# A fused attention and MoE kernel: the second last product as seven products of halves (Strassen), fused with the last one

## The chip, the cores and the metric

The kernel runs on one NeuronCore of one Trainium2 chip. A time is the device time of one execution in microseconds (us). The profile's span runs from the first to the last instruction of one profiled execution and is a little shorter than that execution's time. TensorE (PE in the profile) multiplies matrices; its weight loads are listed apart as PEld. VectorE is DVE, ScalarE is ACT, GpSimd is POOL, SyncE is SP; SP does no arithmetic here and only issues transfers between DRAM and the on-chip memory SBUF. TensorE writes its sums into PSUM, eight banks of 2 KB in each of 128 partitions.

## The reference, cut to what matters

```
p_packed = sm_attn(p, k, v)              # 8 batches, 8 heads, 576 tokens, head size 64
x = sm_attn(q, p_packed, p_packed)       # -> 4608 tokens x 512
x = ((x @ w1) * (x @ w2)) @ w3 @ w_out   # 512 -> 1024 -> 1024 -> 512
h = x @ w_in                             # 4608 x 512 times 512 x 2048: "the second last product"
g = where(h >= 1, h, where(h <= -1, 0, (h + 1)**2 / 4))
out = g @ w_out                          # 4608 x 2048 times 2048 x 512: "the last product"
```

The inputs are float64 or float32, the output is float32. To keep accuracy, each float32 operand of the large products is split into two float32r parts (high and rest), and three of the four products of parts are summed: `PASSES = ((0, 0), (0, 1), (1, 0))`. So one 128x128 piece of weights times one piece of activations costs three matmuls, each with its own weight load.

## The kernel before, in words

The order of the work is written out by hand on every engine; the framework only adds semaphores. There are three stretches.

**Start and batch 0** (to about 178 us): w3 and w_out of the first MoE are multiplied into one matrix, and batch 0 is worked off while weights arrive.

**Batches 1 to 7** (to 607 us): the loop `for b in range(1, B)`. Each batch has 24 units: 16 of `ab_unit` (12 matmuls of 288 columns each) and 8 of `x2_unit` (24 matmuls of 288 columns each), whose results go to the DRAM tensor `x2d`. The steps of the next batch's attention are put between the units. In batches 1 to 6 every fourth unit also calls `wd_convert`: it turns one 128x512 piece of the second MoE's float64 weights (32 pieces: 16 of `win`, 16 of `wout`) into float32 on ScalarE and VectorE and stores it to the DRAM tensor `wd`. In batch 7 the pieces are loaded again and split into their two parts (`wd_split`, one ScalarE and one VectorE instruction each, line 95 and 96), and they stay in SBUF to the end. `x2_block` loads and splits the 512 tokens of a block in the same way.

**The last stretch** (607 us to the end): nine blocks of `TB = 512` tokens, 16 steps each. Step i of a block computes 128 of the 2048 rows of h (`h_step`, line 642: 4 x 3 matmuls of 512 columns into one PSUM bank), and the activation: ScalarE `r` (line 648), VectorE maximum and multiply (lines 650 and 651), and one step later the split of the result into two parts, `g` (lines 95 and 96). Three steps later (`LAG = 3`) `out_step` (line 665) multiplies these parts by one 128-row piece of `wout`: 4 token chunks x 3 matmuls of 512 columns into four PSUM banks that collect over the 16 steps. So TensorE alternates 12 matmuls of `h` and 12 of `o`. At the end of a block ScalarE copies the four banks out (line 672) and issues their stores.

Engines run their queues in order: an instruction that waits holds up everything behind it on its engine. SP's queue of transfers is such a queue too.

Of the kernel before, what the change touches and what calls it, by code (L numbers as in the profile page):

```python
# [8 lines left out]
F32 = mybir.dt.float32  # L9
F32R = mybir.dt.float32r  # L10
# [3 lines left out]
AF = mybir.ActivationFunctionType  # L14
ALU = mybir.AluOpType
# [32 lines left out]
PASSES = ((0, 0), (0, 1), (1, 0))  # L48
# [3 lines left out]
def fused_kernel(ctx: ExitStack, tc, qT, kT, vv, pb, w1, w2, w3T, wo, win, wout, out):  # L52
    nc = tc.nc
# [373 lines left out]
    raw = {}  # L427
# [125 lines left out]
    def wd_load(i):
        if i >= 32:
            return
        if i < 16:
            n, k = divmod(i, 4)
            src = win[k * P:(k + 1) * P, n * 512:(n + 1) * 512]
        else:
            src = wout[(i - 16) * P:(i - 15) * P, :]  # L560
        raw[i] = load_weight(cv, src)

    def wd_convert(i):
        x = cv.tile([P, 512], F32, name="cvx", tag="cvx", bufs=2)
        for f in as_float32(cv, raw.pop(i), x):
            f()
        wd_load(i + 1)
        nc.sync.dma_start(out=wd[i], in_=x)
# [8 lines left out]
    def wd_split(i):
        pool = late["b1"] if i < 16 else late["b2"]
        f = late["b1"].tile([P, 512], F32, name="wf", tag="wf", bufs=3)
        nc.sync.dma_start(out=f, in_=wd[i])  # L580
        w_s[i] = pool.tile([P, 2, 512], F32R, name=f"ws{i}")
        return lambda: split(w_s[i], f)

    def x2_block(t, k):
        b1_, w = late["b1"], late["b1"] if t % 2 == 0 else late["b2"]
        f = b1_.tile([P, TB], F32, name="wf", tag="wf", bufs=3)
        t0 = t * TB
        nc.sync.dma_start(out=f, in_=x2d[t0 // XD][:, k, t0 % XD:t0 % XD + TB])
        x = w.tile([P, 2, TB], F32R, name=f"x2s{k}", tag=f"x2s{k}", bufs=1)
        split(x, f)  # L590
        x2_t[t, k] = x

    for b in range(1, B):
        if b + 1 < B:
            att, sa, bm = attention(b + 1)
            spread = dict(zip(EARLY, att))
            spread.update(zip(LATE, [bm[1, 0], bm[0, 0], sa[0], sa[1], bm[1, 1], bm[0, 1]]))
        else:
            spread = {}
            b1 = late["b1"] = tc.alloc_tile_pool(name="b1", bufs=1, side="left", reuse_waits="tile")  # L600
            todo = [wd_split(i) for i in range(2)]
        seq = []
        for f, n in ((ab_unit, 8), (x2_unit, 4)):
# [28 lines left out]
    todo = [wd_split(16 + i) for i in range(2)]  # L632

    g2_t = {}

    def h_step(t, i):
        ps = psB.tile([P, 512], F32, name="h", tag="h", bufs=2)
# [9 lines left out]
        r = b2.tile([P, TB], F32, name="r", tag="r", bufs=3)  # L647
        nc.scalar.activation(out=r, in_=ps[:, :TB], func=AF.Relu, scale=0.5, bias=half)  # L648
        m = b2.tile([P, TB], F32, name="mx", tag="mx", bufs=3)
        nc.vector.tensor_tensor(out=m, in0=ps[:, :TB], in1=r, op=ALU.max)  # L650
        nc.vector.scalar_tensor_tensor(out=m, in0=r, scalar=1.0, in1=m, op0=ALU.min, op1=ALU.mult)  # L651
        flush()
        g = b2.tile([P, 2, TB], F32R, name="g2", tag="g2", bufs=LAG + 2)
        g2_t[t, i] = g
        pend.append(lambda: split(g, m))

    acc = {}

    def out_step(t, i, cs=range(TB // P)):
        if i == 0:  # L660
            acc[t] = [psB.tile([P, 512], F32, name="o", tag="o", bufs=6) for _ in range(TB // P)]
        g = g2_t[t, i]
        for c in cs:
            for n, (s, v) in enumerate(PASSES):
                nc.tensor.matmul(  # L665
                    acc[t][c], g[:, s, c * P:(c + 1) * P], w_s[16 + i][:, v, :],
                    start=(i == 0 and n == 0), stop=(i == 15 and n == 2),
                )
        if i == 15:
            for c in cs:  # L670
                o = b2.tile([P, DM], F32, name="st", tag="st", bufs=2)
                nc.scalar.activation(out=o, in_=acc[t][c], func=AF.Copy)
                nc.scalar.dma_start(out=out[t * TB + c * P:t * TB + (c + 1) * P, :], in_=o)

    for s in range(16 * NB):
        t, i = divmod(s, 16)
        h_step(t, i)
        if t == 0:
            if i + 2 < 16:
                todo.append(wd_split(18 + i))  # L680
            todo.pop(0)()
        if t + 1 < NB and i >= 8 and i % 2 == 0:
            x2_block(t + 1, i // 2 - 4)
        if LAG <= s < 16 * NB:
            out_step(*divmod(s - LAG, 16))
# [62 lines left out]
```

## Time and profile before

| | us |
|---|---|
| median of three runs | 1402.66 (1401.42 to 1407.57) |
| the profiled execution's own time | 1402.18 |
| its span | 1400.4 |
| TensorE busy in the span | 1358.2 (97%) |
| VectorE busy | 683.9 (49%) |
| ScalarE busy | 477.3 (34%) |
| GpSimd busy | 0.7 |

The page of the profile gives each engine's busy time, the chain of work that ended last (followed back from the last instruction), and groups of instructions by source line with their count and mean duration. A matmul's recorded duration contains the time in which it runs through the array, and consecutive matmuls overlap in it: what one costs is the distance from its start to the next one's start, which the timeline gives. The timeline merges consecutive instructions of one line into a row with a count.

### The profile page before, as it was taken

The page shows a single profiled execution, that of the slowest core. Times are in us where ns is not written, and L with a number is a line of the kernel's source. Part 1 is how long each engine was busy: PE and PEld are TensorE (multiplying, and loading weights), DVE is VectorE, ACT ScalarE, POOL GpSimd, SP SyncE. Part 2 cuts the span into 40 slices and gives each one's busy share as a digit, 9 for nine tenths or more (in the row PEclk, how much of TensorE's full clock was granted, in tenths as well). Part 3 has the DMA queues.
Part 4 walks back from the last instruction along what each step waited for, and adds up shares of the span by engine and source line. Part 5 has one row for each costly group of instructions (what it writes and reads, how often), then busy time and mean ns, then how long its engine had stood idle before and what let it go on. Part 6 is the DMA issues. An engine that isn't in the chain of part 4 may idle for free.

```text
span 1400.4 us, 20204 instructions
## 1 busy us (share of the span) xinstructions
PE 1358.2 (97%) x8280; PEld 1122.6 (80%) x8280; DVE 683.9 (49%) x1269; ACT 477.3 (34%) x945; POOL 0.7 (0%) x6
## 2 busy tenths in 40 slices
PE   6699899999999999999999999999999999999998
PEld 2366688989888898988888888888888888888887
DVE  4684475666665664644434343343433433434332
ACT  3353253444535343533332222322222222222222
POOL 0000000000000000000000000000000000000000
PEclk9799999999999999999999999999999999999999
DMA  8763445536454521421100100001000010000000
GB/s 278 230 211 126 127 152 149 168 117 192 134 156 146 162 96 57 134 89 54 60 31 23 39 15 15 31 23 38 16 15 31 23 38 16 15 31 8 30 1 30
DMA packets 49788, 115.86 MB, mean 83 GB/s; under 512 B 5152, under 2 KB 16416, under 8 KB 47648
## 3 DMA queue, kind: packets, MB, share of 16 engines
q1 hardware_dynamic: 34144, 94.52, 22.1%
q10 hardware_dynamic: 15552, 20.06, 4.0%
q8 instruction: 65, 1.06, 0.3%
q14 instruction: 27, 0.22, 0.0%
HBM read 86.11 MB, written 28.44 MB: 82 GB/s over the span
## 4 chain that ended last, share of the span: by engine, by line
PE 86%; DMA 6%; DVE 4%; SPq 1%; issue 1%; ACT 1%; DVEq 0%; ACTq 0%
PE o L665 28%; PE h L642 28%; PE psk L370 12%; PE psk L394 11%; DMA raw<-win 2%; PE psk L478 2%; DMA raw<-w3T 2%; PE psk L186 2%; PE psm L175 1%; DMA raw<-wout 1%; DMA st<-x2d 1%; SPq L162 1%; PE psm L251 1%; PE psm L225 1%; DMA x2d<-st 1%
## 5 line engine op out<-in xcount | busy, mean ns | idle before, releaser
L665 PE MATMUL o<-ws,g 128*128 128x512 f32 x1728 | 417.7, 391 | 0.0
L642 PE MATMUL h<-x2s,ws 128*128 128x512 f32 x1728 | 417.5, 391 | 0.0
L665 PEld LDWEIGHTS o<-ws,g 128*128 128x128 f32 x1728 | 324.3, 188 | 70.9
L642 PEld LDWEIGHTS h<-x2s,ws 128*128 128x128 f32 x1728 | 324.3, 188 | 69.8 <-DVE x2s L96 0.4
L650 DVE TENSOR_TENSOR mx<-h,r 128x512 f32<-128x512 f32 x144 | 99.5, 691 | 450.2 <-ACT r L648 450.1
L648 ACT ACTIVATE r<-h,half 128x512 f32<-128x512 f32 x144 | 99.1, 688 | 531.5 <-PE h L642 528.2
L394 PEld LDWEIGHTS psk<-g,w 128*128 128x128 f32 x1500 | 200.4, 188 | 25.0 <-ACT st L421 20.7
L370 PE MATMUL psk<-at,m 128*128 128x288 f32 x1494 | 213.7, 298 | 3.8 <-DVE at L321 1.9
L370 PEld LDWEIGHTS psk<-at,m 128*128 128x128 f32 x1494 | 200.5, 188 | 18.2 <-issue 6.7
L394 PE MATMUL psk<-g,w 128*128 128x288 f32 x1500 | 208.8, 297 | 1.2 <-ACT st L421 1.2
L651 DVE SCALAR_TENSOR_TENSOR mx<-r,mx 128x512 f32<-128x512 f32 x144 | 99.7, 692 | 4.9
L96 DVE TENSOR_TENSOR g<-mx,g 128x512 fp32r<-128x512 f32 x144 | 98.4, 683 | 0.1
L382 DVE TENSOR_TENSOR tb<-psk,ta 128x288 f32<-128x288 f32 x124 | 56.3, 455 | 80.5 <-ACT ta L380 37.2
L95 ACT ACTIVATE g<-mx 128x512 fp32r<-128x512 f32 x144 | 89.6, 623 | 1.0 <-DVE mx L651 1.0
L478 PE MATMUL psk<-wo,w3f 128*128 128x512 f32 x128 | 62.7, 641 | 14.1 <-DVE w3f L127 14.1
L116 ACT ACTIVATE cvt<-raw 128x512 f32<-128x512 f32 x72 | 48.3, 675 | 66.7 <-DMA raw<-w 25.6
L380 ACT ACTIVATE ta<-psk 128x288 f32<-128x288 f32 x125 | 50.8, 407 | 51.0 <-PE psk L370 50.0
L478 PEld LDWEIGHTS psk<-wo,w3f 128*128 128x128 f32 x128 | 25.4, 207 | 46.4 <-issue 28.2
L96 DVE TENSOR_TENSOR g<-tb,g 128x288 fp32r<-128x288 f32 x128 | 57.2, 447 | 3.5 <-ACT g L95 2.8
L95 ACT ACTIVATE g<-tb 128x288 fp32r<-128x288 f32 x128 | 56.3, 440 | 6.1 <-DVE tb L382 5.7
L96 DVE TENSOR_TENSOR m<-psk,m 128x512 fp32r<-128x512 f32 x60 | 38.5, 683 | 34.7 <-ACT m L95 34.7
L421 ACT ACTIVATE st<-psk 128x288 f32<-128x288 f32 x61 | 24.8, 406 | 59.7 <-PE psk L394 57.9
(72 smaller groups left out, 602.9 us busy)
## 6 DMA issues: line engine op xcount, KB each, us to landing
x2d<-st ACTq DMA_DIRECT2D x72, 144.0 KB, 2.6
qk<-kT SPq DMA_DIRECT2D x8, 1152.0 KB, 12.3
qk<-qT SPq DMA_DIRECT2D x8, 1152.0 KB, 6.6
wf<-x2d SPq DMA_DIRECT2D x36, 256.0 KB, 2.7
out<-st ACTq DMA_DIRECT2D x36, 256.0 KB, 2.0
raw<-w3T SPq DMA_DIRECT2D x16, 512.0 KB, 5.1
raw<-w SPq DMA_DIRECT2D x16, 512.0 KB, 4.3
raw<-win SPq DMA_DIRECT2D x16, 512.0 KB, 3.9
```

Source lines behind the costliest of these rows:

```text
L95: nc.scalar.activation(out=dst[:, 0], in_=src, func=AF.Copy)
L96: nc.vector.tensor_tensor(out=dst[:, 1], in0=src, in1=dst[:, 0].bitcast(F32), op=ALU.subtract)
L370: nc.tensor.matmul(ps[w][:, :HS], m_tile[b, w, n][:, s, G, c0 * P:(c0 + 1) * P], at_tile[b][:, G, v, hf * HS:(hf + 1) * HS], start=(k == 0 ...
L380: nc.scalar.activation(out=bs, in_=ps[1][:, :HS], func=AF.Copy)
L382: nc.vector.tensor_tensor(out=g, in0=ps[0][:, :HS], in1=bs, op=ALU.mult)
L394: nc.tensor.matmul(ps, w34[kt][:, s, mt * P:(mt + 1) * P], g_t[kt, hf][:, v, :], start=(kt == kts[0] and n == 0), stop=(kt == kts[-1] and ...
L478: nc.tensor.matmul(acc[4 * hf + m], w3f[hf, j][:, m * P:(m + 1) * P], wof[j], start=(j == 0), stop=(j == 7))
L642: nc.tensor.matmul(ps[:, :TB], w_s[4 * n + k][:, s, c0 * P:(c0 + 1) * P], x2_t[t, k][:, v, :], start=(j == 0), stop=(j == 11),)
L648: nc.scalar.activation(out=r, in_=ps[:, :TB], func=AF.Relu, scale=0.5, bias=half)
L650: nc.vector.tensor_tensor(out=m, in0=ps[:, :TB], in1=r, op=ALU.max)
L651: nc.vector.scalar_tensor_tensor(out=m, in0=r, scalar=1.0, in1=m, op0=ALU.min, op1=ALU.mult)
L665: nc.tensor.matmul(acc[t][c], g[:, s, c * P:(c + 1) * P], w_s[16 + i][:, v, :], start=(i == 0 and n == 0), stop=(i == 15 and n == 2),)
```

## The change

The second last product takes, in every block, the matrices in halves: h's two halves of rows, the two halves of the sum's index (512 = 2 x 256), and two halves of 256 tokens (`TH`). Instead of eight products of halves it makes seven, named `A11, S1, A12, S2, S4, S3, A22`, from sums and differences of the quarters of `w_in` and of x (Strassen's scheme in Winograd's form).

- **The products.** A block now has 8 steps in place of 16; a step makes 2 x 128 rows of h. `product` is 6 matmuls of 256 columns (2 pieces x 3 passes), 42 in a step. Three products start a PSUM bank half (`x`, `z`, `y`); the other four add to `x` or `z` after a copy of what stood there was taken: `m1`, `m5`, `u2` on ScalarE. VectorE adds these copies to the banks to make three of the four quarters of the step's h, ScalarE copies the fourth.
- **The last product.** `out_part` is 3 matmuls of 512 columns. The 8 parts (24 matmuls) of step s-1 are placed between the products of step s, in groups of 1, 2, 3 and 2. The activation now reads h from SBUF instead of PSUM.
- **The weights.** `weight_tasks` makes a list of up to 144 tasks, one for each unit of batches 1 to 6: the same 32 conversions, 44 splits (`w_parts`: ScalarE copy, GpSimd subtraction, store of 512 KB; 28 for the seven combinations of `w_in`, 16 for `wout`) and 16 sums or differences on GpSimd (`w_combine`). The parts lie in DRAM (`wid`, `wod`). All 14 parts tiles of `w_in` (1 MB each) are loaded once: six during batch 7, four (`RIGHT`, first half) as soon as batch 7's buffers come free, four more later. A piece of 1 MB of `wout`'s parts is loaded for every step, `wo_load(i + 1)` at the end of step i, into two buffers.
- **The tokens.** A block's 512 tokens come in one load of 1 MB (`x2_load`); seven combinations are split (`x2_parts`, ScalarE and VectorE) after four differences on GpSimd (`x2_combine`). For the next block these 11 tasks are spread over steps 4 to 7.

```diff
--- before.py
+++ after.py
...
+TH = TB // 2
+A11, S1, A12, S2, S4, S3, A22 = range(7)
+LEFT = (A11, S1, A12)
...
-    wd = [dram.tile([P, 512], F32, name=f"wd{i}") for i in range(32)]
+    wid = [[dram.tile([P, 2, 2, 512], F32, name=f"wi{i}{n}") for n in range(2)] for i in range(7)]
+    wod = [dram.tile([P, 2, 2, DM], F32, name=f"wo{i}") for i in range(8)]
...
+    def w_convert(key, nxt):
+        def f():
+            x = wx[key] = cv.tile([P, 512], F32, name="cvx", tag="cvx", bufs=4)
+            for f in as_float32(cv, raw.pop("w"), x):
+                f()
+            if nxt is not None:
+                w_raw(nxt)
+        return f
+    def w_parts(key, dst):
+        def f():
+            x = wx[key]
+            p = cv.tile([P, 2, 512], F32R, name="hl", tag="hl", bufs=1)
+            nc.scalar.activation(out=p[:, 0], in_=x, func=AF.Copy)
+            nc.gpsimd.tensor_tensor(out=p[:, 1], in0=x, in1=p[:, 0].bitcast(F32), op=ALU.subtract)
+            nc.sync.dma_start(out=dst, in_=p.bitcast(F32))
+        return f
+    def w_combine(key, a, b, op):
+        return lambda: nc.gpsimd.tensor_tensor(out=wx[key], in0=wx[a], in1=wx[b], op=op)
+    def weight_tasks():
...
+        lines = [[conv.pop(0) for _ in range(3)], [conv.pop(0)]]
+        for x, (k, n) in enumerate(groups):
+            q = {z: (x, z) for z in (11, 12, 21, 22)}
+            take = lambda m=1: [conv.pop(0) for _ in range(m) if conv]
+            part = lambda i, z: w_parts(q[z], wid[i][n][:, k])
+            lines.append([part(A11, 11), None, None])
+            lines.append([part(A22, 22), w_combine(q[22], q[21], q[22], ALU.add), None])
+            lines.append([part(A12, 12), None, None])
+            lines.append([part(S1, 22), w_combine(q[22], q[22], q[11], ALU.subtract),
+                          w_combine(q[21], q[11], q[21], ALU.subtract)])
+            lines.append([part(S2, 22), w_combine(q[12], q[12], q[22], ALU.subtract)] + take())
+            lines.append([part(S3, 21)] + take())
+            lines.append([part(S4, 12)] + take() + take())
+            for j in range(4 * x, 4 * x + 4):
+                lines.append([w_parts(("o", j), wod[j // 2][:, j % 2])] + take())
...
+    def wi_load(i, n):
+        t = wi_t[i, n] = late["b1" if i in LEFT else "b2"].tile([P, 2, 2, 512], F32R, name=f"wi{i}{n}")
+        nc.sync.dma_start(out=t.bitcast(F32), in_=wid[i][n])
...
+    def x2_load(t):
+        f = late["b1"].tile([P, 4, TB], F32, name="f", tag="f", bufs=1)
         t0 = t * TB
+        nc.sync.dma_start(out=f, in_=x2d[t0 // XD][:, :, t0 % XD:t0 % XD + TB])
+        for r in range(2):
+            for c in range(2):
+                x2f[10 * r + c + 11] = f[:, 2 * r:2 * r + 2, c * TH:(c + 1) * TH]
+    def x2_combine(dst, a, b):
+        return lambda: nc.gpsimd.tensor_tensor(out=x2f[dst], in0=x2f[a], in1=x2f[b], op=ALU.subtract)
+    def x2_parts(t, i, src):
+        def f():
+            x = late["b1"].tile([P, 2, 2, TH], F32R, name="x2s", tag="x2s", bufs=8)
+            x2_t[t, i] = x
+            nc.scalar.activation(out=x[:, 0], in_=x2f[src], func=AF.Copy)
+            nc.vector.tensor_tensor(out=x[:, 1], in0=x2f[src], in1=x[:, 0].bitcast(F32), op=ALU.subtract)
+        return f
+    def x2_tasks(t):
+        return [
+            x2_parts(t, A11, 11), x2_combine(11, 12, 11), x2_combine(12, 22, 12),
+            x2_parts(t, S1, 11), x2_parts(t, A12, 21),
+            x2_parts(t, S4, 22), x2_combine(22, 22, 11),
+            x2_parts(t, S2, 22), x2_combine(21, 21, 22),
+            x2_parts(t, S3, 12), x2_parts(t, A22, 21),
+        ]
...
+            x2_load(0)
+            for n in range(2):
+                for i in LEFT:
+                    wi_load(i, n)
+            x2_todo = x2_tasks(0)
...
             if b == B - 1:
+                for _ in range(2 if u >= 18 else 0):
+                    if x2_todo:
+                        x2_todo.pop(0)()
+            elif w_todo:
+                task = w_todo.pop(0)
+                if task:
+                    task()
...
+    def wo_load(i):
+        t = wo_t[i] = buf("wo")
+        nc.sync.dma_start(out=t.bitcast(F32), in_=wod[i])
+    RIGHT = [i for i in range(7) if i not in LEFT]
+    first["g2"] = buf("g2")
+    late_wi = []
+    for i in RIGHT[:2]:
+        t = wi_t[i, 1] = b2.tile([P, 2, 2, 512], F32R, name=f"wi{i}1")
+        late_wi.append((t, i))
+    for i in RIGHT:
+        wi_load(i, 0)
+    for tag in ("H", "r"):
+        first[tag] = buf(tag)
+    wo_load(0)
+    for tag in ("m1", "m5", "u2", "st"):
+        first[tag] = buf(tag)
+    for i in RIGHT[2:]:
+        t = wi_t[i, 1] = b2.tile([P, 2, 2, 512], F32R, name=f"wi{i}1")
+        late_wi.append((t, i))
+    for t, i in late_wi:
+        nc.sync.dma_start(out=t.bitcast(F32), in_=wid[i][1])
...
+    BANK = {A11: "x", S1: "z", A12: "y", S2: "x", S4: "z", S3: "x", A22: "x"}
...
+    def product(t, i, q):
+        b = BANK[q]
+        if q in (A11, S1, A12):
+            bank[b] = psB.tile([P, TH], F32, name=b, tag=b, bufs=2 if b == "x" else 1)
         n, c0 = divmod(i, 4)
         j = 0
-        for k in range(4):
+        for k in range(2):
             for s, v in PASSES:
                 nc.tensor.matmul(
-                    ps[:, :TB], w_s[4 * n + k][:, s, c0 * P:(c0 + 1) * P], x2_t[t, k][:, v, :],
-                    start=(j == 0), stop=(j == 11),
+                    bank[b], wi_t[q, n][:, k, s, c0 * P:(c0 + 1) * P], x2_t[t, q][:, v, k, :],
+                    start=(j == 0 and q in (A11, S1, A12)), stop=(j == 5), skip_group_check=True,
                 )
                 j += 1
...
+    def copy(tag, b):
+        c = buf(tag)
+        nc.scalar.activation(out=c, in_=bank[b], func=AF.Copy)
+        return c
+    def activation(src):
+        r = buf("r")
+        nc.scalar.activation(out=r, in_=src, func=AF.Relu, scale=0.5, bias=half)
+        nc.vector.tensor_tensor(out=src, in0=src, in1=r, op=ALU.max)
+        nc.vector.scalar_tensor_tensor(out=src, in0=r, scalar=1.0, in1=src, op0=ALU.min, op1=ALU.mult)
+        g = buf("g2")
+        pend.append(lambda: split(g, src))
+        return g
+    def evacuate(t, c):
+        o = buf("st")
+        nc.scalar.activation(out=o, in_=acc.pop(c), func=AF.Copy)
+        nc.scalar.dma_start(out=out[t * TB + c * P:t * TB + (c + 1) * P, :], in_=o)
+    def out_part(t, i, h, c):
+        if i == 0 and h == 0:
+            acc[c] = psB.tile([P, DM], F32, name="o", tag="o", bufs=4)
+        for n, (s, v) in enumerate(PASSES):
+            nc.tensor.matmul(
+                acc[c], g2_t[t, i, h][:, s, c * P:(c + 1) * P], wo_t[i][:, h, v, :],
+                start=(i == 0 and h == 0 and n == 0), stop=(i == 7 and h == 1 and n == 2),
+            )
+        if i == 7 and h == 1:
+            evacuate(t, c)
+    g2_t = {}
+    for s in range(8 * NB):
+        t, i = divmod(s, 8)
+        todo = x2_tasks(t + 1) if i == 4 and t + 1 < NB else todo if s else []
+        outs = [(h, c) for h in range(2) for c in range(TB // P)] if s else []
...
+        product(t, i, A11)
+        m1 = copy("m1", "x")
+        product(t, i, S1)
+        m5 = copy("m5", "z")
+        product(t, i, A12)
+        H = [buf("H"), buf("H")]
+        nc.vector.tensor_tensor(out=H[0][:, :TH], in0=bank["y"], in1=m1, op=ALU.add)
         flush()
...
+        tasks(2 if i == 7 else 0)
+        some(1)
+        product(t, i, S2)
+        u2 = copy("u2", "x")
+        product(t, i, S4)
+        nc.vector.tensor_tensor(out=H[0][:, TH:], in0=bank["z"], in1=u2, op=ALU.add)
+        g2_t[t, i, 0] = activation(H[0])
+        some(2)
+        product(t, i, S3)
+        nc.vector.tensor_tensor(out=H[1][:, TH:], in0=bank["x"], in1=m5, op=ALU.add)
+        flush()
+        tasks(2 if i == 7 else 0)
+        some(3)
+        tasks(2 if i == 7 else 0)
+        product(t, i, A22)
+        nc.scalar.activation(out=H[1][:, :TH], in_=bank["x"], func=AF.Copy)
+        g2_t[t, i, 1] = activation(H[1])
+        tasks(9 if i == 7 else 1 if i >= 4 else 0)
+        some(2)
+        if i == 2 and t + 1 < NB:
+            x2_load(t + 1)
+        if s + 1 < 8 * NB:
+            wo_load((i + 1) % 8)
     flush()
     for c in range(TB // P):
-        for i in range(16 - LAG, 16):
-            out_step(NB - 1, i, (c,))
+        for h in range(2):
+            out_part(NB - 1, 7, h, c)
```

## Rows read from the trace of the kernel before

**Rows 1.** The page: busy time of each engine; the chain that ended last, by line.

```profile
PE 1358.2 (97%) x8280; PEld 1122.6 (80%) x8280; DVE 683.9 (49%) x1269; ACT 477.3 (34%) x945; POOL 0.7 (0%) x6
PE o L665 28%; PE h L642 28%; PE psk L370 12%; PE psk L394 11%; DMA raw<-win 2%; PE psk L478 2%; DMA raw<-w3T 2%; PE psk L186 2%; PE psm L175 1%; DMA raw<-wout 1%; DMA st<-x2d 1%; SPq L162 1%; PE psm L251 1%; PE psm L225 1%; DMA x2d<-st 1%
```

**Rows 2.** Stretches: window; length; PE, PEld, DVE, ACT, POOL busy; clock; DMA share; GB/s.

```profile
300.00:400.00 100.00, 99.25 (x958) 87.97 (x957) 62.70 (x140) 46.12 (x110) 0.00 (x0) 1.00 0.50 152
900.00:1000.00 100.00, 100.00 (x440) 82.22 (x439) 39.52 (x61) 26.62 (x45) 0.00 (x0) 1.00 0.07 22
```

**Rows 3.** Timeline, TensorE alone: start, duration, line, operation, count; batch 7's end.

```profile
581.89 25.55 PE L394 MATMUL psk<-g,w 128*128 128x288 f32 x192
607.28 11.33 PE L642 MATMUL h<-x2s,ws 128*128 128x512 f32 x48
```

**Rows 4.** Timeline of the kernel's end.

```profile
1385.81 11.08 PE L665 MATMUL o<-ws,g 128*128 128x512 f32 x48
1396.93 0.60 ACT L672 ACTIVATE st<-o 128x512 f32<-128x512 f32 x1 [1.44 <-PE o L665]
```

**Rows 5.** Lines, their weight loads: count, duration in ns (min/median/max), forms.

```profile
L251 PEld LDWEIGHTS psm<-v,et x640: 106/110/177, 43.2 to 514.5; 116*32 116x32 f32 x128, 112*32 112x32 f32 x32
L175 PEld LDWEIGHTS psm<-qk,pb x128: 132/136/137, 15.0 to 502.0; 128*64 128x64 f32 x128
L394 PEld LDWEIGHTS psk<-g,w x1500: 186/188/269, 100.0 to 607.0; 128*128 128x128 f32 x188
```

**Rows 6.** Groups by line: count, busy us, mean ns, then idle time before them.

```profile
L272 ACT ACTIVATE ppt<-psm 128x128 f32<-128x128 f32 x4 | 1.1, 278 | 0.4
L380 ACT ACTIVATE ta<-psk 128x288 f32<-128x288 f32 x125 | 50.8, 407 | 51.0 <-PE psk L370 50.0
L259 DVE TENSOR_TENSOR pp<-psm,rd 128x128 f32<-128x128 f32 x4 | 1.2, 292 | 1.6 <-PE psm L251 1.6
L382 DVE TENSOR_TENSOR tb<-psk,ta 128x288 f32<-128x288 f32 x124 | 56.3, 455 | 80.5 <-ACT ta L380 37.2
L651 DVE SCALAR_TENSOR_TENSOR mx<-r,mx 128x512 f32<-128x512 f32 x144 | 99.7, 692 | 4.9
L96 DVE TENSOR_TENSOR g<-mx,g 128x512 fp32r<-128x512 f32 x144 | 98.4, 683 | 0.1
L95 ACT ACTIVATE g<-mx 128x512 fp32r<-128x512 f32 x144 | 89.6, 623 | 1.0 <-DVE mx L651 1.0
```

**Rows 7.** Timeline of the last stretch, all engines: from matmuls to ScalarE and VectorE.

```profile
903.50 2.88 PE L665 MATMUL o<-ws,g 128*128 128x512 f32 x12
903.76 0.69 ACT L648 ACTIVATE r<-h,half 128x512 f32<-128x512 f32 x1 [4.26 <-PE h L642]
904.48 0.69 DVE L650 TENSOR_TENSOR mx<-h,r 128x512 f32<-128x512 f32 x1 [3.45 <-ACT r L648]
```

**Rows 8.** Loads: issue, count, KB, us to landing; then a stretch near the start, as Rows 2.

```profile
qk<-qT SPq DMA_DIRECT2D x8, 1152.0 KB, 6.6
10.00:15.00 5.00, 5.00 (x8) 1.73 (x6) 1.94 (x5) 0.85 (x2) 0.00 (x0) 1.00 1.01 412
```

**Rows 9.** Tile raw, 180 to 560 us: who waited for it (us, times); loads' landing.

```profile
  DVE cvx L121: 26.9, 5
  ACT cvt L116: 23.2, 5
  PEld psm L175: 0.8, 5
DMA to landing us min/median/max: 3.8/3.9/15.3
```

**Rows 10.** Timeline, TensorE alone: the same matmuls in batch 3 and in batch 4.

```profile
336.98 12.86 PE L394 MATMUL psk<-g,w 128*128 128x288 f32 x96
400.50 12.86 PE L394 MATMUL psk<-g,w 128*128 128x288 f32 x96
```

More of the change, by code (lines that the diff above doesn't have):

```diff
@@ L550, in fused_kernel @@
         emit(steps[k])
[L553 to L568, printed above, removed]
@@ L570, in fused_kernel @@
-    raw.clear()
-    wd_load(0)
-    wd_next = 0
-    w_s = {}
-    x2_t = {}
[L577 to L586, printed above, removed]
-        t0 = t * TB
[L588 to L591, printed above, removed]
+    wx = {}
@@ new lines, in fused_kernel, with w_raw @@
+    w_todo = []
+    def w_raw(src):
+        raw["w"] = load_weight(cv, src)
+    def w_convert(key, nxt):
[14 more added lines that the diff above has]
+        return f
@@ new lines, in w_combine @@
+    def w_combine(key, a, b, op):
+        return lambda: nc.gpsimd.tensor_tensor(out=wx[key], in0=wx[a], in1=wx[b], op=op)
+    def weight_tasks():
+        groups = [(k, n) for n in range(2) for k in range(2)]
+        seq = []
+        for x, (k, n) in enumerate(groups):
+            for r, c in ((0, 0), (1, 1), (1, 0), (0, 1)):
+                seq.append(win[(2 * c + k) * P:(2 * c + k + 1) * P, (2 * r + n) * 512:(2 * r + n + 1) * 512])
+            for j in range(4 * x, 4 * x + 4):
+                r = (j % 2) * 8 + j // 2
+                seq.append(wout[r * P:(r + 1) * P, :])
+        conv = [lambda: w_raw(seq[0])]
+        nxt = seq[1:] + [None]
+        conv = []
+        for x in range(4):
+            for q in (11, 22, 21, 12):
+                conv.append(w_convert((x, q), nxt[len(conv)]))
+            for j in range(4 * x, 4 * x + 4):
+                conv.append(w_convert(("o", j), nxt[len(conv)]))
+        lines = [[conv.pop(0) for _ in range(3)], [conv.pop(0)]]
+        for x, (k, n) in enumerate(groups):
+            q = {z: (x, z) for z in (11, 12, 21, 22)}
[9 more added lines that the diff above has]
+            lines.append([part(S4, 12)] + take() + take())
+            for j in range(4 * x, 4 * x + 4):
+                lines.append([w_parts(("o", j), wod[j // 2][:, j % 2])] + take())
+        out = []
+        for l in lines:
+            out += (l + [None, None, None])[:3]
+        assert not conv
+        w_raw(seq[0])
+        return out
@@ L631, in fused_kernel, with buf @@
     psB = tc.alloc_tile_pool(name="psB", bufs=1, space=PSUM, reuse_waits="tile")
[L632 to L637, printed above, removed]
+    KINDS = {
+        "g2": ([P, 2, TB], F32R, 4), "H": ([P, TB], F32, 3), "r": ([P, TB], F32, 2), "wo": ([P, 2, 2, DM], F32R, 2),
+        "m1": ([P, TH], F32, 2), "m5": ([P, TH], F32, 2), "u2": ([P, TH], F32, 2), "st": ([P, DM], F32, 2),
+    }
+    first = {}
+    def buf(tag):
+        if tag in first:
+            return first.pop(tag)
+        shape, dtype, bufs = KINDS[tag]
+        return b2.tile(shape, dtype, name=tag, tag=tag, bufs=bufs)
@@ L638, in h_step @@
+    for i in RIGHT[2:]:
[4 more added lines that the diff above has]
+    BANK = {A11: "x", S1: "z", A12: "y", S2: "x", S4: "z", S3: "x", A22: "x"}
+    acc = {}
+    bank = {}
+    def product(t, i, q):
+        b = BANK[q]
+        if q in (A11, S1, A12):
+            bank[b] = psB.tile([P, TH], F32, name=b, tag=b, bufs=2 if b == "x" else 1)
         n, c0 = divmod(i, 4)
@@ L646, in h_step @@
                 j += 1
[L647 to L651, printed above, removed]
-        flush()
-        g = b2.tile([P, 2, TB], F32R, name="g2", tag="g2", bufs=LAG + 2)
@@ L654, in h_step @@
[L654 to L685, printed above, removed]
+    def copy(tag, b):
[10 more added lines that the diff above has]
+        return g
@@ new lines, in fused_kernel, with some, tasks @@
+    g2_t = {}
[3 more added lines that the diff above has]
+        outs = [(h, c) for h in range(2) for c in range(TB // P)] if s else []
+        def some(n):
+            for _ in range(n):
+                if outs:
+                    out_part(*divmod(s - 1, 8), *outs.pop(0))
+        def tasks(n):
+            for _ in range(n):
+                if todo:
+                    todo.pop(0)()
+        product(t, i, A11)
[5 more added lines that the diff above has]
+        nc.vector.tensor_tensor(out=H[0][:, :TH], in0=bank["y"], in1=m1, op=ALU.add)
+        flush()
+        tasks(2 if i == 7 else 0)
[21 more added lines that the diff above has]
+            wo_load((i + 1) % 8)
```

16 lines of the change are left out of this document (5 added, 11 removed).

## The prediction

> **What bounds the kernel now.** I read the page's shares first: TensorE is busy for 97% of the span, and the two matmul lines of the last stretch alone hold 56% of the chain that ended last [rows 1]. The stretches come next: from 900 to 1000 us TensorE never idles, at a granted clock of 1.00, while VectorE is busy 40% and ScalarE 27%; in batch 3 TensorE is busy 99%, VectorE 63%, ScalarE 46% [rows 2]. So every stretch that the change touches is bounded by the matmul stream, and the question is what one matmul costs. Durations don't tell it, distances do. From the start of the last stretch to the start of the last group of `o` there are 3408 matmuls of 512 columns in 1385.81 - 607.28 = 778.5 us: **228.4 ns** each [rows 3, 4]. The last 192 matmuls of 288 columns took 607.28 - 581.89 = 25.39 us: **132.2 ns** each [rows 3]. Streaming alone, at 2.4 GHz, would be 213.3 and 120.0 ns, so each matmul with its weight load costs 12 to 15 ns more than its columns.
>
> **What 256 columns will cost.** No matmul of this form with 256 columns is in the trace. The line through the two measured points gives 132.2 - 32 x (228.4 - 132.2) / 224 = 118.5 ns; columns plus the smaller extra give 106.7 + 12.2 = 118.9. I take **119**. The lower bound is the columns alone, 107; the upper is 132, the time of the 288-column one, if something other than columns sets its pace. The candidate is the weight load: its record grows from 110 ns for 32 weight columns over 136 for 64 to 188 for 128 [rows 5], some 0.82 ns a column, so 128 columns need about 105 ns of pure loading (estimate). That is just under the 107 ns of streaming 256 columns: at 288 and 512 columns the load has room, at 256 it has none. I stay with 119 because both measured sizes agree with columns plus a constant.
>
> The Trainium skill (TensorE: Matmul & The Clock Gate, section Back-to-back issue gap) gives columns / 2.4 + 2.5 ns. By that a 512-column matmul would take 215.8 and a 288-column one 122.5; the rows have 228.4 and 132.2, so the measurement decides; that rule's 109 ns stands below as a rival. Its section on LDWEIGHTS gives 107 ns for 128 columns, near my 105.
>
> **Last stretch, TensorE.** Before, two steps are 48 x 228.4 = 10.963 us. After, one step has 42 matmuls of 256 and 24 of 512: 42 x 119 + 24 x 228.4 = 4.998 + 5.482 = **10.480 us**. The gain is 0.48 us a step, 35 us over 72 steps, and 1 ns more on the short matmul takes back 42 x 72 = 3024 ns.
>
> **Is each step covered?** A 256-column copy on ScalarE lies between 278 (128 columns) and 407 ns (288), by line 381; a VectorE add from PSUM between 292 and 455, by line 422 [rows 6]. ScalarE then works 4 x 0.38 + 2 x 0.69 + 2 x 0.62 = 4.1 us of a step, VectorE 3 x 0.42 + 2 x (0.69 + 0.69 + 0.68) = 5.4: both have room. The waits: ScalarE starts 0.26 us after the last matmul's slot (903.50 to 903.76), VectorE 0.03 after ScalarE [rows 7]. The tightest is `A22`, which adds to bank `x` and must wait for VectorE's addition of `m5`, which is queued behind the activation of `H[0]`. Counted from a step's start: S4 ends at 5 x 0.714 + 0.685 = 4.26; H[0]'s second half 4.52 to 4.94, r to 5.66, maximum to 6.38, multiply to 7.07, addition of `m5` to 7.49. `A22` is due after S3 and six of eight parts: 4.26 + 1.37 + 0.71 + 2.06 = 8.40. It has 0.9 us to spare; `S2`, `S4` and `S3` have 1 to 2 us after their copies. I cost the waits of steps 1 to 71 at nothing; without this cover each 0.1 us costs 7 us.
>
> **What is not covered.** (1) Step 0 has no parts of `o` between its products: `A22` comes due at 4.3 us and its addition is done at about 6.7 (the same chain from S4's end at 3.6), so 2.5 us are lost and the step takes 7.5. (2) At each of the 8 block changes step 7 carries six more splits on ScalarE and VectorE and a chain S4 split, GpSimd difference, S2 split, which ScalarE meets ahead of the copy of `H[1]` and of the next step's `m1`. GpSimd's price for 512 elements isn't in the trace (it made 6 instructions, 0.7 us in all [rows 1]); VectorE's for the same operation, 0.68 us [rows 6], is the lower bound, four times that, 2.7, my upper one; I take 1.4, twice VectorE's. Then `m1` is done some 1.0 us after `S2` is due: 1.0 x 8 = 8 us (0 to 20). (3) At the end, 24 matmuls remain after the last step (5.5 us) and the second half's activation, 4.3 us from `A22`'s end, is covered by 2.1 us of matmuls only: I take 2.0 lost. (4) From the last matmul's end to the span's end nothing changes: 1400.4 - 1396.9 = 3.5 [rows 4].
>
> On (2): the Trainium skill (SBUF — State Buffer, section Who interferes with whom) says that a VectorE instruction with two SBUF inputs and a GpSimd instruction that reads SBUF hold each other up for the whole instruction. No run here shows it yet; with one difference of 1.4 us at most in the way, it would add up to 1.4 us to a block change, 11 us in all, within the 0 to 20 above.
>
> **Transfers.** A step loads 1 MB of `wout`'s parts, one step ahead; 1152 KB took 6.6 us to land and the core has moved up to 412 GB/s [rows 8], so 1 MB in 10.5 us is covered, with 4 us to spare. Only the change of stretch is tight: `wo(1)` is queued on SP behind `wo(0)` and four `w_in` tiles that wait for batch 7's last buffers, 6.3 MB from 607.3 on. At 330 to 412 GB/s they land 17 to 21 us later; `wo(1)` is due 7.5 + 10.5 + 2.1 = 20 us later. I take 1 us (0 to 8).
>
> **Batches 1 to 7.** Batch 7 loses 18 splits from engines that are off the path: nothing. Batches 1 to 6 (378 us) get 44 copies of 0.62 = 27 us more on ScalarE, 60 GpSimd instructions, 14 MB more stores, and conversions that now stand one or two units apart instead of four. TensorE has slack for lone delays: 10 waits of about 5 us on `raw` (50 us on ScalarE and VectorE) cost its weight loads 0.8 us [rows 9]. But with one `raw` buffer, 3.9 us to land (15.3 behind a larger load) and units of 2.6 us (the same matmuls come 63.5 us later in the next batch of 24 units [rows 10]), ScalarE will stand more often, and `w_parts` with one buffer `hl` can hold it too, until the store has landed; behind it stand the copies that free TensorE's banks. I take **5 us** (0 to 20).
>
> **The sum**, against the profiled execution: before, 1400.4 - 607.3 = 793.1 us for the last stretch. After: 7.5 + 71 x 10.480 (744.1) + 8 + 5.5 + 2.0 + 3.5 + 1 = 771.6. Gain 21.5, less 5 in the batches: 16.5. The span becomes 1383.9; with 1402.18 - 1400.4 = 1.8 us around it, 1385.7. The profiled execution lies 0.5 us under the median, so nothing is corrected: **1386 us**. Its own range: 116 to 123 ns (-9 to +12), block changes (-8 to +8), batches (-5 to +5), not all at once: 1370 to 1402.
>
> **Rivals.** (B) *The weight load becomes the pace of the 256-column matmul.* For it: the estimate of 105 ns leaves no room. Against it: constant extra at two sizes. It decides at 119 + 16.5 / 3.024 = 124.5 ns, above which the change loses; at 126 to 132 ns the time is 1407 to 1425. (C) *The products wait for their banks.* `A22`'s 0.9 us are the sum of seven durations; if the chain is 1.3 us longer, each step loses 0.4 us, 71 x 0.4 = 28: 1414 (1400 to 1430). (D) *The weight tasks show in batches 1 to 6*, 15 to 30 us instead of 5: 1396 to 1411; for it the single buffers, against it the 0.8 us of before. (E) *The extra over the columns vanishes at 256*, so that a short matmul costs 109 ns: 10 x 3.024 = 30 us less, 1356; against it the extra at both measured sizes. (It is what the Trainium skill's rule above gives.)
>
> **How the numbers follow.** Chances: forecast 0.56, B 0.17, C 0.12, D 0.10, E 0.05. About 0.5% (7 us) is what a measurement of this kernel can tell from no change. Faster than 1395.6: 0.50 of the forecast, E, a little of D: 0.57. Within: 0.06 of the forecast, 0.03 of B, 0.04 of C, 0.08 of D: 0.21. Slower: 0.22. The range 1362 to 1414 leaves out most of E, half of B and half of C, 0.19.
>
> **What would show it.** Right: starts of 256-column matmuls 116 to 122 ns apart, steps of about 10.5 us without idle TensorE, the last stretch at 770 us, its start at 612. Wrong: 126 ns or more with no idle time (B); idle time before `A22` or `S2` in every step, released by VectorE or ScalarE (C); the last stretch starting after 620 (D); waits on `wo`'s transfers in every step, which I exclude.

## The result, and the profile after

| | before | changed kernel |
|---|---|---|
| median, us | 1403.1 (1401.4 to 1407.6, 4 runs) | 1425.9 (1419.5 to 1426.6, 4 runs) |
| ratio, 95% interval | | 1.0147 (1.0110 to 1.0185) |
| profiled execution, span | 1402.18, 1400.4 | 1425.31, 1423.5 |
| batches 1 to 6 in it | 175.8 to 556.5: 380.7 | 172.1 to 603.2: 431.1 |
| batch 7 | 50.8 | 50.8 |
| last stretch | 607.3 to 1400.4: 793.1 | 654.0 to 1423.5: 769.5 |

The change made the kernel 1.5% slower. The last stretch became 23.6 us shorter, close to the forecast; batches 1 to 6, which compute nothing new but prepare the weights, became 50.4 us longer (the 3.7 us by which batch 1 starts earlier make up the rest of the difference). Batch by batch it is +11.7, +11.5, +17.1, +5.6, +1.6 and +2.9 us. The page of the changed kernel, shares and chain by engine (as [rows 1]):

```profile
PE 1335.9 (94%) x9576; PEld 1163.8 (82%) x9576; DVE 801.6 (56%) x1480; ACT 618.3 (43%) x1272; POOL 129.4 (9%) x102
PE 68%; DVE 11%; DMA 10%; ACT 5%; issue 2%; POOL 1%; SPq 1%; ACTq 1%; DVEq 0%; POOLq 0%
```

The windows of [rows 2], changed kernel:

```profile
300.00:400.00 100.00, 83.70 (x744) 73.04 (x744) 58.23 (x111) 42.16 (x95) 19.77 (x15) 0.91 0.46 160
900.00:1000.00 100.00, 98.84 (x621) 88.61 (x620) 57.51 (x96) 46.79 (x91) 8.09 (x6) 1.00 0.33 116
```

From 300 to 400 us TensorE is busy 84% where it was 99%, and the mean granted clock is 0.91: it idles, and comes back at the lower level. Over batches 1 to 6 it idles for 41.5 us (3.4 before), and the same matmuls keep it busy for 389.6 us (377.3 before) at a mean granted clock of 0.96 (1.00 before): of the 50.4 us, 38.1 are idle time and 12.3 slower matmuls. No other engine is full there (VectorE 58%, ScalarE 42%): it is waits, not work. TensorE's share of the chain fell from 86% to 68%; transfers hold 10%, VectorE 11%.

The names in the next rows: `raw` is a piece of weights as it was loaded, `cvt` and `cvx` its conversion, `hl` the two parts of a piece ahead of their store (to `wi` or `wo`). `psk` and `psm` are PSUM banks, `ta` is a copy that frees a bank, and `big` are the attention's transposes, which free `psm`. The longest of these waits, in the timeline of the changed kernel (start, duration, engine, line, tiles; idle time of the engine before, and who ended it; rows in between are left out):

```profile
347.79 2.43 PE L377 MATMUL psk<-at,m 128*128 128x288 f32 x17
347.87 0.28 SPq L168 DMA_DIRECT2D v<-vv  x1
348.19 4.48 SPq L169 DMA_DIRECT2D v<-vv  x1
349.30 0.70 ACT L123 ACTIVATE cvt<-raw 128x512 f32<-128x512 f32 x1 [1.97 <-DMA raw<-wout]
350.80 3.45 PE L377 MATMUL psk<-at,m 128*128 128x288 f32 x24
353.99 0.35 SPq L109 DMA_DIRECT2D raw<-wout  x1
366.05 0.67 ACT L123 ACTIVATE cvt<-raw 128x512 f32<-128x512 f32 x1 [15.42 <-DMA raw<-wout]
366.06 0.46 DVE L128 TENSOR_SCALAR cvx<-raw 128x512 uint16<-128x512 uint16 x1 [14.42 <-DMA raw<-wout]
366.62 0.39 ACT L387 ACTIVATE ta<-psk 128x288 f32<-128x288 f32 x1
369.29 1.22 PE L193 MATMUL psm<-qk,ppt 64*32 64x288 f32 x16 [15.04 <-DVE big L295]
```

SP issues v's load at 348 to 353 and a raw piece of `wout` right behind it, at 354.0. The piece lands at 366, 12 us later instead of 4. Its conversion was already at the head of ScalarE's and VectorE's queues, so both stood for 15 us. VectorE's transposes `big` stood behind it; TensorE's next matmuls, a step of the attention, waited for them, and TensorE idled for 15.0 us, then went on at a granted clock of 0.50 (369.3 to 373.0 us). The waits of this stretch in the changed kernel, summed (who for whom: us, times, longest):

```profile
ACT cvt L123 <- DMA raw<-wout: 31.3, 7, 15.4
ACT cvt L123 <- DMA raw<-win: 16.8, 6, 10.1
ACT hl L585 <- DMA wi<-hl: 24.9, 6, 7.8
ACT hl L585 <- DMA wo<-hl: 6.6, 4, 3.5
```

And all waits for the tile raw in it, as in [rows 9]:

```profile
  ACT cvt L123: 48.1, 13
  DVE cvx L128: 39.9, 12
```

In [rows 9] it was 5 waits each, 23.2 and 26.9 us, and TensorE's weight loads lost 0.8 us.

### The profile page after: what moved, and what is told of

It reads as the page before. It is cut to its first block, busy times and chain, and to the rows that moved or that the text cites. A ratio compares the mean times of both kernels' runs of the same rounds, so it can differ in the third digit from the quotient of the medians.

```text
span 1423.5 us, 23629 instructions
## 1 busy us (share of the span) xinstructions
PE 1335.9 (94%) x9576; PEld 1163.8 (82%) x9576; DVE 801.6 (56%) x1480; ACT 618.3 (43%) x1272; POOL 129.4 (9%) x102
## 4 chain that ended last, share of the span: by engine, by line
PE 68%; DVE 11%; DMA 10%; ACT 5%; issue 2%; POOL 1%; SPq 1%; ACTq 1%; DVEq 0%; POOLq 0%
PE o L795 24%; PE x L765 13%; PE psk L401 9%; PE psk L377 9%; PE z L765 6%; PE y L765 3%; DMA raw<-wout 2%; DMA wi<-hl 2%; DMA raw<-w3T 2%; DMA raw<-win 1%; PE psk L193 1%; DVE g L103 1%; PE psk L485 1%; DMA wo<-hl 1%; ACT r L778 1%
## 5 line engine op out<-in xcount | busy, mean ns | idle before, releaser
L795 PE MATMUL o<-wo,g 128*128 128x512 f32 x1728 | 441.3, 391 | 1.3 <-ACT g L102 1.3
L795 PEld LDWEIGHTS o<-wo,g 128*128 128x128 f32 x1728 | 304.7, 188 | 48.5 <-ACT g L102 1.7
L765 PEld LDWEIGHTS x<-x2s,wi 128*128 128x128 f32 x1728 | 243.2, 189 | 36.4 <-ACT m L773 12.4
L765 PE MATMUL x<-x2s,wi 128*128 128x256 f32 x1728 | 252.1, 282 | 7.7 <-ACT m L773 5.3
L779 DVE TENSOR_TENSOR H<-H,r 128x512 f32<-128x512 f32 x144 | 99.7, 692 | 182.5 <-ACT r L778 182.5
L778 ACT ACTIVATE r<-H,half 128x512 f32<-128x512 f32 x144 | 104.2, 724 | 66.3 <-DVE H L831 64.0
L765 PE MATMUL z<-x2s,wi 128*128 128x256 f32 x864 | 125.0, 281 | 0.0
L103 DVE TENSOR_TENSOR g<-H,g 128x512 fp32r<-128x512 f32 x144 | 103.6, 720 | 29.8 <-ACT g L102 29.8
L765 PEld LDWEIGHTS z<-x2s,wi 128*128 128x128 f32 x864 | 112.0, 191 | 0.0
L780 DVE SCALAR_TENSOR_TENSOR H<-r,H 128x512 f32<-128x512 f32 x144 | 99.7, 692 | 4.9
```

Source lines behind the costliest of these rows:

```text
L765: nc.tensor.matmul(bank[b], wi_t[q, n][:, k, s, c0 * P:(c0 + 1) * P], x2_t[t, q][:, v, k, :], start=(j == 0 and q in (A11, S1, A12)), stop ...
L778: nc.scalar.activation(out=r, in_=src, func=AF.Relu, scale=0.5, bias=half)
L779: nc.vector.tensor_tensor(out=src, in0=src, in1=r, op=ALU.max)
L780: nc.vector.scalar_tensor_tensor(out=src, in0=r, scalar=1.0, in1=src, op0=ALU.min, op1=ALU.mult)
L795: nc.tensor.matmul(acc[c], g2_t[t, i, h][:, s, c * P:(c + 1) * P], wo_t[i][:, h, v, :], start=(i == 0 and h == 0 and n == 0), stop=(i == 7 ...
```

## The experiments

The first theory (L): the 32 conversions, now up to four in consecutive units, stand at the head of ScalarE's and VectorE's queues until their raw piece has landed. Its rivals: H, ScalarE stands at the splits for the one buffer `hl`; Q, SP stands at the stores until GpSimd is done (229 us in all), so that q, k and v come late; E, the added work itself. All but the last two runs leave the last stretch as it is. "Batches" is the time of batches 1 to 6 in the profiled execution.

| run | median us (runs) | ratio to before (95%) | batches | last stretch |
|---|---|---|---|---|
| changed kernel | 1425.9 (4) | 1.0147 (1.0110 to 1.0185) | 431.1 | 769.5 |
| raw_once | 1383.9 (2) | 0.9864 (0.9816 to 0.9911) | 387.3 | 770.7 |
| copy_pool | 1427.5 (2) | 1.0174 (1.0127 to 1.0221) | 430.9 | 768.6 |
| store_pool | 1420.2 (2) | 1.0122 (1.0071 to 1.0173) | 420.4 | 768.3 |
| spread | 1405.2 (10) | 1.0018 (0.9996 to 1.0041) | 411.2 | 767.9 |
| v_pool | 1409.8 (8) | 1.0045 (1.0025 to 1.0065) | 406.4 | 768.7 |
| spread_v_pool | **1372.0** (4) | 0.9786 (0.9771 to 0.9801) | 382.6 | 768.5 |
| spread_store_pool | 1405.2 (10) | 1.0026 (1.0011 to 1.0041) | 410.4 | 769.9 |
| spread_sub_dve | 1403.1 (8) | 1.0006 (0.9980 to 1.0031) | 403.6 | 770.2 |
| before_v_pool | 1395.5 (4) | 0.9943 (0.9925 to 0.9960) | 378.3 | 793.4 |
| x2_early | 1377.8 (4) | 0.9837 (0.9801 to 0.9874) | 381.4 | 770.5 |
| x2_early_evac | 1386.4 (4) | 0.9874 (0.9845 to 0.9903) | 382.4 | 781.0 |

**No waits for raw pieces.**

```
-            for f in as_float32(cv, raw.pop("w"), x):
+            for f in as_float32(cv, raw["w"], x):
                 f()
-            if nxt is not None:
-                w_raw(nxt)
```

> Leaves out all but the first load of w_in's and w_out's raw pieces: each of the 32 conversions reads the piece that already stands in the one buffer, so no conversion waits for a transfer; conversions, splits, GpSimd work and stores stay. Batches 1 to 6 took 431 us (172.1 to 603.2) in the changed kernel and 381 in the one before. Theory L (ScalarE and VectorE stand at conversions until their piece has landed): 395 us or less, the last stretch starts near 618. Theory H (ScalarE stands at the splits for the one buffer hl): 415 to 430. Theory Q (SP stands at the stores, so q, k and v come late): 410 to 430, the long waits move to the attention's matmuls. Theory E (the added work on ScalarE and GpSimd itself): 425 to 431.

387.3 us: 43.8 of the 50.4 are gone, and the last stretch starts at 613. Theory L holds, E and H fall: all work, splits and stores are there, and ScalarE's waits for `hl` too (33 us with those for `wo`, 31.5 in the changed kernel). The run also takes 31 loads out of SP's queue; spread_v_pool below keeps them all and is faster still, so it is the waits that count, not the loads' traffic.

```profile
ACT hl L583 <- DMA wi<-hl: 22.0, 7, 7.0
ACT hl L583 <- DMA wo<-hl: 11.2, 5, 6.3
```

**GpSimd makes the copy.**

```
-            nc.scalar.activation(out=p[:, 0], in_=x, func=AF.Copy)
+            nc.gpsimd.tensor_copy(out=p[:, 0], in_=x)
```

> The copy into hl's first half is made by GpSimd in place of ScalarE, so only GpSimd waits for the one buffer hl, and ScalarE has 27 us less to do. Batches 1 to 6, 431 us in the changed kernel: theory H: 395 or less. Theory L: 415 to 431, the waits on raw stay. Theory Q: 425 to 435, since SP waits for GpSimd longer than before. Theory E: 400 if ScalarE's load is what counts, over 431 if GpSimd's is.

430.9 us, no change: as long as the raw pieces are waited for, neither the waits for `hl` nor 27 us of ScalarE's work count (its waits for raw pieces grew from 48 to 63 us).

**Stores from GpSimd's queue.**

```
-            nc.sync.dma_start(out=dst, in_=p.bitcast(F32))
+            nc.gpsimd.dma_start(out=dst, in_=p.bitcast(F32))
```

> The 44 stores of parts are issued from GpSimd's own queue in place of SP's, so SP's queue holds loads alone and never waits for a subtraction (it did for 229 us in all). Batches 1 to 6, 431 us in the changed kernel: theory Q: 400 or less, raw pieces land in 4 us more often. Theory L: 410 to 425, as only those loads that stood behind a store get earlier. Theory H: 425 to 435. Theory E: 431.

420.4 us, 11 less: what L expected. Q is not the main cause.

**The tasks in another order** (in part; these lines take the place of the list `lines`).

```
+            at = dict(zip((0, 4, 8, 12, 18, 22, 27, 31), conv[8 * x:8 * x + 8]))
+            at.update({2: part(A11, 11), 6: part(A22, 22), 9: w_combine(q[22], q[21], q[22], ALU.add), ...
+            for u, task in at.items():
+                out[36 * x + u] = task
```

> The same 92 tasks over the same 144 units, in another order: conversions 4 or 5 units apart as in the kernel before (there 4), splits 2 to 4 apart, mostly 3. Nothing is left out. Theory L: batches 1 to 6 fall from 431 to 385 to 395 us and the time to 1380 to 1390, under the kernel before. Theory H: 415 to 425, time about 1415, since splits stand no further apart. Theory Q: 420 to 430, since as many stores stand in SP's queue. Theory E: 431, since the work is the same.

411.2 us: 20 of the 50, half of what L expected. ScalarE's waits for raw pieces are gone (0.7 us), those for `hl` are left (37 us), the longest where a store of `hl` stands behind v's load. SP and ScalarE in that run:

```profile
203.74 0.27 SPq L168 DMA_DIRECT2D v<-vv  x1
204.06 4.65 SPq L169 DMA_DIRECT2D v<-vv  x1
209.60 1.18 SPq L587 DMA_DIRECT2D wi<-hl  x1
...
225.42 0.63 ACT L585 ACTIVATE hl<-cvx 128x512 fp32r<-128x512 f32 x1 [6.82 <-DMA wi<-hl]
```

So the theory changed (V): what is late is whatever stands behind v's load in SP's queue, once in every batch; the order of the tasks decides who waits for it.

**v's load on another queue.** In v_pool with the changed kernel's order, in spread_v_pool with the new order:

```
-        nc.sync.dma_start(out=t[:, :n], in_=vv[b, :n * CH].rearrange("(c p) d -> p c d", p=CH))
-        nc.sync.dma_start(out=t[:CHS[n], n], in_=vv[b, n * CH:])
+        (nc.gpsimd if b > 1 else nc.sync).dma_start(out=t[:, :n], in_=vv[b, :n * CH].rearrange("(c p) d -> p c d", p=CH))
+        (nc.gpsimd if b > 1 else nc.sync).dma_start(out=t[:CHS[n], n], in_=vv[b, n * CH:])
```

> Batches 2 to 7's load of v (928 and 224 KB, 18 to 19 us from issue to landing, 4.7 us to issue) goes from SP's queue to GpSimd's; all else as in the changed kernel. Theory V (raw pieces and stores land in 10 to 15 us where they stand behind v's load in SP's queue, in 3 to 4 otherwise): batches 1 to 6 fall from 431 to 400 us or less. Rival (too little distance between a load and its conversion, whatever lies before it): 420 or more. Rival (GpSimd, which now also issues v, holds up the subtractions): over 431.

> The spread order and v's load on GpSimd's queue together. Theory V: what is left in the spread order (411 us against 381 in the kernel before) are stores and loads behind v's load, so batches 1 to 6 take 383 to 392 us and the whole 1378 to 1390. Rival (GpSimd's work and the two-input instructions of VectorE that it holds up): 405 or more, about 1400.

v_pool: 406.4 us in its profiled execution, 25 less, between the two expectations. That execution, 1397.5 us, was the fastest of eight; by the medians the edit is worth 16 us (1425.9 to 1409.8). ScalarE still stands 34 us at conversions there, up to 9.2 us at a time, so the short distance between a load and its conversion, the first rival, counts as well. spread_v_pool: 382.6 us, 1.9 more than before the change, and 1372.0 us in all, **2.1% under the kernel before**. By the medians v's queue is worth 33 us in the new order (1405.2 to 1372.0); the order is worth 21 us with v on SP's queue (1425.9 to 1405.2) and 38 with it moved (1409.8 to 1372.0): each does more once the other is put right. v still takes 22 us to land there; only the queue that it stands in is another. v's load in that run, and a window (as [rows 2]):

```profile
v<-vv POOLq DMA_DIRECT2D x6, 928.0 KB, 22.5
```

```profile
300.00:400.00 100.00, 99.56 (x951) 89.01 (x951) 71.06 (x141) 50.66 (x120) 29.36 (x23) 1.00 0.59 194
```

TensorE is back at 99.6% and clock 1.00. The Trainium skill (DMA: Bandwidth & Descriptors, section Rules for kernel authors) says that spreading transfers over the issuing engines doesn't help bandwidth and only saves the issuing time; here one load on another queue was worth 16 and 33 us by the medians, since others no longer stood behind it. The same page's section on queues and rings, where descriptors are consumed in ring order, agrees with that.

**Stores from GpSimd's queue, new order.** The two edits of spread and store_pool together.

> The spread order with the 44 stores on GpSimd's queue, v's load stays on SP's. Theory V: the stores no longer stand behind v's load, raw pieces still do: batches 1 to 6 take 390 to 400 us, the whole 1385 to 1395. Rival (GpSimd's work itself): 405 or more.

410.4 us: no gain, theory V's number missed. The stores now all land in 3 to 8 us, but ScalarE's waits for `hl` hardly fall (36 us against 37 in spread): 13 of up to 5.5 us in place of 11 of up to 8.6. `pp`, a step of the attention, holds TensorE six times (11.6 us). With v on SP's queue, a queue of their own for the stores added nothing to the new order; why `pp` waits more here is open.

**Subtractions on VectorE, new order.**

```
-            nc.gpsimd.tensor_tensor(out=p[:, 1], in0=x, ...
+            nc.vector.tensor_tensor(out=p[:, 1], in0=x, ...
```

> The spread order with the 44 subtractions on VectorE in place of GpSimd (which keeps the 16 combinations). Theory V: 405 to 411 us for batches 1 to 6, a little less since a part is ready for its store about 1 us earlier. Rival (VectorE's instructions with two SBUF inputs are held up by GpSimd's: line 103's mean went from 447 to 583 ns): 395 or less, and that mean falls back to about 460.

403.6 us and 508 ns for line 103: between the two. GpSimd's work does lengthen VectorE's two-input instructions (447 ns in the kernel before, 583 in the changed one), as the Trainium skill has it (SBUF — State Buffer, section Who interferes with whom), but it is not what costs the time: in spread_v_pool, with all of GpSimd's work, that mean is 566 ns, and the batches take 382.6 us.

**The kernel before with v on GpSimd's queue.** The same edit as in v_pool.

> The kernel before with batches 2 to 7's load of v on GpSimd's queue, nothing else. Theory V with slack: before the change, loads behind v's were late too (13.8 and 15.3 us) but ScalarE's waits of about 5 us cost TensorE under 1 us, so the time stays within 3 us of 1403 and the gain of the spread kernel with v on GpSimd's queue is the change's. Rival (v's place on the queue was worth as much to the kernel before): 1385 to 1395.

1395.5 us, a gain of 7 us, more than expected and 0.5 us short of the rival: 2.4 in the batches, 5 ahead of them (batch 1 starts at 171.1 instead of 175.8). The second part is v's too: at the end of batch 0 the loads of partial sums, `st`, stand behind batch 2's v in SP's queue, VectorE waits for them, and TensorE for VectorE. In the kernel before:

```profile
161.14 0.46 DVE L419 TENSOR_TENSOR st<-psk,st 128x288 f32<-128x288 f32 x1 [8.62 <-DMA st<-x2d]
162.50 1.21 PE L186 MATMUL psm<-qk,ppt 64*32 64x288 f32 x16 [5.74 <-DVE big L288]
```

With v moved this wait of TensorE is gone. So of the 31 us between spread_v_pool and the kernel before, 7 belong to v and some 23.5 to the change itself, about the last stretch's gain (793.4 to 768.5).

**Two edits at the block changes**, both on top of spread_v_pool:

```
         flush()
-        tasks(2 if i == 7 else 0)
+        tasks(4 if i == 7 else 0)
         some(1)
...
         some(3)
-        tasks(2 if i == 7 else 0)
```

> Spread order and v on GpSimd's queue as before (1372.0), and in step 7 the split of S4's tokens and the GpSimd difference after it move ahead to the first group of tasks, the second pair ahead of the last parts of o. Theory: the 0.5 us of each block's step 7 (10.92 us against 10.42) is the ScalarE copy of S2 that waits for that difference; it goes, 8 x 0.5 = 4 us: 1368. The next step's 0.65 us (11.07) stays. Rival: VectorE then reaches the addition for A22 late and the time moves to another wait of step 7: 1372 or more.

The rival: the wait moved. Counted from the start of `A11`, the 0.5 us lie in a block's first step and the 0.65 in its second, both ahead of `S2`, which waits for `m1` (the expectations name the step before). Here the first step takes 10.42 us instead of 10.92 and the second 10.75 instead of 11.07, but the last step of a block takes 11.48 instead of 10.42, as `A22` now waits for VectorE. The last stretch takes 770.5 us against 768.5. TensorE's waits from 700 to 1350 us, and one block change:

```profile
PE x L762 <- DVE H L832: 5.6, 7, 0.8
```

```profile
1105.12 3.00 POOL L652 TENSOR_TENSOR f<-f 128x512 f32<-128x512 f32 x2 [21.07 <-DVE x2s L659]
1106.99 1.67 DVE L777 SCALAR_TENSOR_TENSOR H<-r,H 128x512 f32<-128x512 f32 x1
```

VectorE's multiply, which has two inputs in SBUF and lies ahead of the addition that `A22` waits for, takes 1.66 to 1.67 us in each of seven blocks, with GpSimd's two differences running at the same time, and 0.69 elsewhere. That is 1.0 us of the 1.6 by which the addition is late; the earlier splits alone would have left it within `A22`'s cover of 0.9 us (estimate from these durations).

The second one also moves the copies of `o` for `c >= 2` to VectorE (`nc.vector.tensor_copy`).

> As the one with the earlier split, and the last two of a block's four copies of o go from ScalarE to VectorE. Theory: the 0.65 us of each block's step 0 are ScalarE's wait for an out buffer ahead of the copy m1; they go, 8 x 0.65 = 5 us more, 1363. Rival: VectorE, which now waits for that buffer, holds up the activation instead: no gain on the one before.

No gain, as the rival had it, but by another way: 781.0 us. VectorE makes the two copies after the activation and without a wait of its own; ScalarE, which still issues their stores, stands until they are made, and `m1` is behind it. The block's second step takes 11.87 us instead of 10.75. ScalarE's waits from 700 to 1350 us:

```profile
ACT m L770 <- DVE st L787: 21.8, 7, 3.4
```

## Why the prediction was wrong

The forecast was 1386 us; 1426 came, outside the range. Taken step by step, the last stretch came out about right and the batches were wrong.

**The price of a short matmul: right.** A step of the changed kernel, TensorE alone:

```profile
1043.19 0.88 PE L765 MATMUL x<-x2s,wi 128*128 128x256 f32 x6
1043.91 0.88 PE L765 MATMUL z<-x2s,wi 128*128 128x256 f32 x6
1044.63 0.88 PE L765 MATMUL y<-x2s,wi 128*128 128x256 f32 x6
1045.34 0.86 PE L795 MATMUL o<-wo,g 128*128 128x512 f32 x3
...
1053.61 0.88 PE L765 MATMUL x<-x2s,wi 128*128 128x256 f32 x6
```

(1045.34 - 1043.19) / 18 = 119 ns, as taken from columns plus a constant; the next step starts 10.42 us later (10.48 forecast). Rival B is out: the weight load hides under 256 columns. Rival E is out as well, and with it the 109 ns of the Trainium skill's rule, which its section gives for an isolated matmul.

**The covers: right.** No wait shows from a block's third step to its last, each 10.42 us, so rival C is out. `A22` had the 0.9 us of the forecast (addition done at 1050.67, `A22` at 1051.55 in the step above), and that is what x2_early overran.

**The uncovered places: about right in sum.** Step 0 took 7.67 us (7.5), and its stall has the place that the prediction named:

```profile
657.58 0.90 PE L765 MATMUL x<-x2s,wi 128*128 128x256 f32 x6
660.87 1.80 PE L765 MATMUL x<-x2s,wi 128*128 128x256 f32 x12 [2.39 <-DVE H L835]
662.47 1.48 PE L765 MATMUL z<-x2s,wi 128*128 128x256 f32 x6
```

After it six matmuls take 1.28 us instead of 0.72 for a while: the next step took 11.98 us, 1.6 more than the others, which the prediction had not counted. A block change costs 1.13 us (1.0 forecast, GpSimd's 512 elements 1.37 us against 1.4 taken), but by two mechanisms: 0.5 in the new block's first step, where `S2` waits for `m1` as described, and 0.65 in its second step, where ScalarE stands for an out buffer ahead of `m1`; that one the prediction had missed, and that the term came out at its size is luck. The end lost 1.5 us (2.0), the loads of `wout`'s parts none (1). Sum: 769.5 against 771.6; the steps, each 0.06 us shorter than forecast, paid for what was missed.

**Batches 1 to 6: wrong.** The step that failed is the term "5 us (0 to 20)": it measured 50.4, of which 12.3 are matmuls at a lower granted clock, a cost that the prediction did not count at all. The prediction named the mechanism (one buffer, denser conversions, a piece behind a larger load at 15.3 us, ScalarE's queue ahead of the banks), and priced it by the kernel before, where 10 such waits cost TensorE 0.8 us. That price does not carry over. In the kernel before a piece had four units, 10.5 us, to land, so a landing of 15 us left 5 us of standing, and TensorE had enough queued to bridge that. In the changed kernel the next conversion is often one unit, 2.6 us, away. Ten of ScalarE's 13 waits then came with pieces that landed within 5.4 us of their issue, and behind v's load ScalarE stood for 10.1 and 15.4 us. What of this reaches TensorE is no fixed share. Under the 10.1 us TensorE still had 48 matmuls of `x2_unit` to do (6.5 us) and lost 4.5; at the 15.4 us and at a wait of 3.2 an attention step that needs the standing engine came next, and TensorE lost 15.0 and 4.5. raw_once shows that these waits are 44 of the 50 us; v_pool and spread_v_pool show that the long landings come from v's load ahead in the queue. Rival D (15 to 30 us) had the right place and too small a price; its ends, and the bound of 20, had no row behind them.

What stays open: how the last 6.6 us of raw_once's batches divide among `hl`, GpSimd's hold on VectorE and the added work; and why `pp` waits more in spread_store_pool.

## What to carry to other kernels

A wait that costs nothing today is covered up to a point: price a change by the distance that it leaves between a load and its use (here 10.5 us before, 2.6 at the shortest after) against the worst landing in that queue (up to 16 us), not by what the wait cost before. What lies beyond can reach TensorE in full, as 15.0 us of 15.4 did, and bring slower matmuls with it. Preparing data in the gaps of a tuned stretch is only free if a load is issued farther ahead than the slowest transfer of its queue takes; a slow load that nobody waits for belongs on a queue with nothing urgent behind it. And the arithmetic saving was real: with both put right, the same seven products gave 1372 us.

## What the runs showed of the hardware that was not expected

In all eleven runs with the seven products TensorE stops for 2.4 us at the same place of the first step. In five of them (the changed kernel, raw_once, spread_store_pool, spread_sub_dve, x2_early_evac) the granted clock then fell to 0.50, the 1.2 GHz level, for some 3.5 us, with matmuls of 256 columns 213 ns apart, and the next step took 11.9 to 12.0 us; in the other six it stayed at 1.00, and that step took 10.43. The stops of under 1 us at a block change were not followed by a lower clock. In batches 1 to 6 of the changed kernel, 38 us more of idle time came with 12 us of slower matmuls, so idle time there cost more than itself. And 512 KB that land in 3.9 us took 11 to 16 us behind 1.15 MB of v, which itself needs up to 4.8 us of SP's time to issue and 16 to 20 us to land.
